# Moving the output stores of the opening and the end from SyncE's DMA queue to GpSimd's, in a fused window-attention and MLP kernel

## The chip, the cores and the metric

One core of one Trainium2 chip. The metric is device time in microseconds (us) of one execution. The trace of an execution gives the span from its first to its last instruction; the time of that same execution is about 1.7 us longer than its span.

The profile's names: PE is TensorE, DVE VectorE, ACT ScalarE, POOL GpSimd, SP SyncE. Of TensorE's work, `h_ps` is the first MLP layer, `o_ps` the second, `sc` and `pv` are the two products of attention, `tp` transposes. The granted clock is the share of TensorE's full clock that the records of a trace show. GELU is ScalarE's activation of the first layer. In these traces a DMA tells of its landing by 16 increments of a semaphore, a counter that engines wait for.

## The reference

Attention over a window of 32 positions to each side, 8 batches of 8 heads, 576 positions, head size 64, and then a two-layer MLP on the 4608 tokens that come out:

```python
def _attn_ref(q, k, v):                       # (8, 8, 576, 64) each
    scores = np.matmul(q, k.transpose(0, 1, 3, 2)) / np.sqrt(64)
    mask = np.abs(pos[:, None] - pos[None, :]) <= 32
    ...                                       # masked softmax
    return np.matmul(attn, v)

def _moe_ref(x, w_in, w_out):                 # x (4608, 512), w_in (512, 2048), w_out (2048, 512)
    h = x @ w_in
    g = h * (1.0 / (1.0 + np.exp(-1.702 * h)))
    return (g @ w_out).astype(np.float32)
```

## The kernel before

Tokens are handled in 36 units of 128. After an opening ("head") that fills the pipeline, each "window" computes attention for two units, the first layer for two units before them and the second layer for two more. An output tile `o_sb` (128 x 512, float32) is stored in two DMAs of 128 KB. Inside the kernel the rows are permuted by four (`JT = 4`), so a store's access pattern starts with a dimension of 4:

```python
    def stores(self, eng):
        while self.o_sb:
            u, o_sb = self.o_sb.pop(0)
            row = 128 * u + 32
            for blk in range(2):
                eng.dma_start(self.out[row + 64 * blk:row + 64 * blk + 64, :].rearrange("(s j) f -> j s f", j=JT),
                                  o_sb[64 * blk:64 * blk + 64])
```

The windows of the steady state store through GpSimd (52 DMAs). SyncE (SP) stores units 0 to 3 in the opening (8 DMAs) and units 30 to 34 at the end (10). SP also issues all DMA transposes, in program order; the one of key block 12 comes right behind the opening's stores:

```python
        run(1)
        self.stores(nc.sync)          # units 0 to 3, on SP
        self.load_v(8)                # loads are issued by GpSimd
        self.load_v(9)
        self.load_v(10)
        self.load_k(12)
        self.load_heads(3, "q")
        self.layer1(2, 0)
        ...
        self.load_v(11)
        self.load_v(12)
        self.load_k(13)
        self.keys_X(12)               # nc.sync.dma_start_transpose(self.kT[...], ...)
```

The last unit (`layer2_last`) stores each half as soon as it is copied, through SP and ScalarE. That is not changed.

The softmax here doesn't subtract the row's maximum and nothing guards it: scores larger than these inputs give would overflow.

Of the kernel before, what the change touches and what calls it, by code (L numbers as in the profile page):

```python
# [21 lines left out]
JT = 4  # L22
# [5 lines left out]
class _Kernel:  # L28
# [305 lines left out]
            self.cast(eng or nc.vector, o_sb, o_ps)  # L334
            self.o_sb.append((u, o_sb))

    def stores(self, eng):
        while self.o_sb:
            u, o_sb = self.o_sb.pop(0)
            row = 128 * u + 32  # L340
            for blk in range(2):
                eng.dma_start(self.out[row + 64 * blk:row + 64 * blk + 64, :].rearrange("(s j) f -> j s f", j=JT),  # L342
                                  o_sb[64 * blk:64 * blk + 64])

    def layer2_last(self):

# [26 lines left out]
    def head(self):  # L373

        nc, dve, act, pool = self.nc, self.nc.vector, self.nc.scalar, self.nc.gpsimd
# [91 lines left out]
        def run(n):  # L467
            for _ in range(n):
                l2.pop(0)()
# [23 lines left out]
        run(1)  # L493
        self.x_T(5, "a", act)
        run(1)
        self.stores(nc.sync)
        self.load_v(8)
        self.load_v(9)
        self.load_v(10)
        self.load_k(12)  # L500
        self.load_heads(3, "q")
        self.layer1(2, 0)
        self.values(6)
        self.norm(6)
# [15 lines left out]
    def window(self, w):  # L520
        nc, dve, sp = self.nc, self.nc.vector, self.nc.sync
        a, b = 2 * w, 2 * w + 1
        att = w < self.NW
        eng = {0: dve, 1: nc.scalar}
        l2 = [(lambda u=u, i=i: self.layer2(u, i, "oa"[u % 2] if w == self.NW else "oh"[u % 2], eng[u % 2]))
              for u in (2 * w - 4, 2 * w - 3) for i in range(4) if u < self.NU - 1]
        l1 = [(lambda d=d: self.layer1(w - 1, d)) for d in range(8)] if w <= self.NW else []

        def run(lst, n=1):
            for _ in range(min(n, len(lst))):  # L530
                lst.pop(0)()

        def loads():
            for m in (2 * w + 4, 2 * w + 5):
                if 12 < m < self.NU:
                    self.keys_X(m)
            for m in (2 * w + 5, 2 * w + 6):
                if m < self.NU:
                    self.load_v(m)
                if m + 1 < self.NU:  # L540
                    self.load_k(m + 1)
            if w % 2 == 0 and 512 * (w // 2 + 2) < self.N:
                self.load_heads(w // 2 + 2, "q")

        if w == 4:
            self.scores(7)
            self.scores(a)
            run(l2, 3)
            self.band(7)
            self.scores(b)  # L550
            run(l2)
            self.band(a)
            self.values(7)
            self.norm(7)
            self.gelu_table()
            self.band(b)
            run(l2, 2)
            self.values(a)
            run(l2)
            self.values(b)  # L560
            self.x_T(7, "t", nc.scalar)
            self.norm(a)
            self.x_T(a)
            self.norm(b)
            self.x_T(b)
            loads()
            self.keys_wrap()
            run(l2)
            run(l1, 2)
            for hp in range(4):  # L570
                self.pair_heads("q", 3, hp, dve)
            run(l1, 2)
            for hp in range(4):
                self.queries_T(3, hp, "t", nc.scalar)
                run(l1)
            self.feed(w)
            return
        self.stores(nc.gpsimd if att else nc.sync)
        loads()
        if att:  # L580
            self.scores(a)
            if w > 5:
                self.scores(b)
        run(l2, 2)
        if w == 5:
            self.scores(b)
        run(l2)
        if att:
            self.gelu_table()
            self.band(a)  # L590
            self.band(b)
        run(l2)
        run(l2, 2)
        if att:
            self.values(a)
            self.values(b)
            self.norm(a)
            self.x_T(a)
            self.norm(b)
            self.x_T(b)  # L600
        run(l2, 0 if w == self.NW else 2)
        if w > self.NW:
            self.stores(nc.sync)
            self.layer2_last()
        run(l1, 4)
        self.feed(w)
        run(l1, 4)
        run(l2, 2)
        if w >= self.NW - 1:
            self.stores(nc.sync)  # L610

    def feed(self, w):

# [68 lines left out]
```

## Time and profile before

| | before |
|---|---|
| time, median of 3 runs | 318.3 us (318.05 to 319.51) |
| span of the traced run, and its time | 314.7 us, 316.4 us |
| TensorE busy | 95% |
| chain that ended last | TensorE 89% |
| opening stores on SP | 8, issued from 52.0 us |
| end stores on SP | 10, the last two from 306.64 us |

TensorE is the bound: a change in DMA traffic shows in the time only where TensorE waits for it. Two lines of SP's timeline are added here, because the prediction read them wrongly (columns: start us, duration us, engine, line, operation, tiles, count):

```profile
52.00 7.46 SPq L342 DMA_DIRECT2D out_dram<-o_sb  x8
59.57 4.74 SPq L148 DMA_TRANSPOSE kT<-kn  x1
```

The second is the key transpose. Its issue starts as soon as the eight stores are issued and takes 4.74 us, where most later transposes take 1.2 to 1.6.

### The profile page before, as it was taken

How to read it: one execution, taken by the hardware profiler on the slowest of the kernel's cores; microseconds unless marked ns; L12 is line 12 of the kernel's file. 1: busy time of each engine (PE TensorE's matmuls, PEld its weight loads, DVE VectorE, ACT ScalarE, POOL GpSimd, SP SyncE). 2: the span in 40 equal slices, each digit the busy share in tenths (PEclk: the TensorE clock that was granted, in tenths of full speed). 3: DMA queues.
4: the chain of work that ended last, by engine and by line, in shares of the span. 5: the costliest groups of instructions: out<-in, count | busy, mean ns of one | idle time of the engine just before them, and what ended most of it. 6: DMA issues, size and time to landing. Idle time of an engine off the chain costs nothing.

```text
span 314.7 us, 8731 instructions
## 1 busy us (share of the span) xinstructions
PE 298.3 (95%) x3719; PEld 205.0 (65%) x3754; DVE 122.4 (39%) x373; ACT 189.0 (60%) x302; POOL 120.4 (38%) x173
## 2 busy tenths in 40 slices
PE   7999999995999999999999999999999999999993
PEld 4678655852857585858584848585858575757762
DVE  3581068454335334442435252616160707070001
ACT  3476364790785757566666667676757575765330
POOL 8993455413616361736171617161612202000000
PEclk9999999997999999999999999999999999999999
DMA  7999999999996999899989999999999222202103
GB/s 130 154 193 200 196 188 177 178 85 133 107 83 110 154 162 118 121 151 181 97 125 131 182 114 126 142 192 92 130 136 124 49 57 52 52 19 73 46 21 79
DMA packets 128238, 38.22 MB, mean 121 GB/s; under 512 B 108744, under 2 KB 125384, under 8 KB 128200
## 3 DMA queue, kind: packets, MB, share of 16 engines
q0 software_dynamic: 87424, 25.08, 89.3%
q1 hardware_dynamic: 40680, 12.53, 33.0%
q8 instruction: 29, 0.48, 0.7%
q10 hardware_dynamic: 96, 0.07, 0.1%
q14 instruction: 9, 0.07, 0.1%
HBM read 36.96 MB, written 9.44 MB: 147 GB/s over the span
## 4 chain that ended last, share of the span: by engine, by line
PE 89%; ACT 4%; issue 3%; DVE 1%; DMA 1%; ACTq 0%
PE h_ps L319 39%; PE o_ps L330 37%; PE sc L244 4%; PE pv L280 3%; PE tp L168 2%; PE junk L370 1%; PE o_ps L356 1%; DMA k_raw<-in_k_dram 1%; ACT p L252 1%; ACT qT L103 1%; ACT p L250 1%; ACT g L321 1%; PE tp L307 1%; PE tp L165 1%; DVE x L292 1%
## 5 line engine op out<-in xcount | busy, mean ns | idle before, releaser
L319 PE MATMUL h_ps<-xT,w_in_sb 128*128 128x256 bf16 x1152 | 130.9, 273 | 0.0
L330 PE MATMUL o_ps<-w_out_sb,g 128*128 128x512 bf16 x525 | 122.9, 381 | 7.9 <-issue 7.5
L319 PEld LDWEIGHTS <-w_in_sb 128*128 128x128 bf16 x1152 | 111.8, 98 | 16.7 <-DVE xT L103 0.3
L321 ACT ACTIVATE g<-h_ps 128x512 bf16<-128x512 f32 x144 | 85.9, 597 | 45.6 <-PE h_ps L319 45.5
L330 PEld LDWEIGHTS <-g 128*128 128x128 bf16 x560 | 51.6, 98 | 61.4 <-issue 4.3
L342 POOL DMA_DIRECT2D out_dram<-o_sb x52 | 33.1, 640 | 114.6 <-DVE o_sb L103 77.3
L264 DVE TENSOR_TENSOR p<-p,mask 128x512 bf16<-128x512 bf16 (+1 forms) x74 | 30.0, 413 | 101.8 <-ACT p L250 99.2
L137 POOL DMA_DIRECT2D ve<-in_v_dram x40 | 34.8, 875 | 12.4 <-DMA w_out_sb<-in_moe_w_out_dram 4.0
L250 ACT ACTIVATE p<-sc 128x512 bf16<-128x512 f32 (+1 forms) x74 | 36.7, 579 | 3.5 <-PE sc L244 3.3
L103 ACT COPY o_sb<-o_ps 128x512 f32<-128x512 f32 x15 | 8.8, 586 | 38.7 <-PE o_ps L330 38.7
L292 DVE TENSOR_TENSOR x<-pv,rec 128x256 bf16<-128x256 f32 x72 | 30.6, 425 | 2.5
L144 POOL DMA_DIRECT2D kn<-in_k_dram x27 | 23.6, 879 | 8.0 <-DMA ve<-in_v_dram 5.3
L103 DVE COPY o_sb<-o_ps 128x512 f32<-128x512 f32 x20 | 13.6, 686 | 24.4 <-PE o_ps L330 24.4
L291 DVE RECIPROCAL rec<-pv 128x4 f32<-128x4 f32 x72 | 12.6, 175 | 20.1 <-PE pv L280 20.1
L250 ACT ACT_TABLE_LOAD x15 | 19.2, 1283 | 0.3
L364 ACT ACT_TABLE_LOAD x14 | 18.0, 1283 | 0.2
L280 PEld LDWEIGHTS <-p 128*64 128x64 bf16 x576 | 11.4, 113 | 9.1 <-issue 7.1
L103 DVE COPY kT<-tp 128x512 bf16<-128x512 bf16 (+1 forms) x13 | 8.5, 659 | 21.4 <-PE tp L168 20.7
L103 ACT COPY qT<-tp 128x512 bf16<-128x512 bf16 (+1 forms) x16 | 9.1, 572 | 11.8 <-PE tp L168 10.7
L131 POOL DMA_DIRECT2D qs<-in_q_dram x17 | 12.3, 732 | 8.6 <-DMA ve<-in_v_dram 5.0
L244 PEld LDWEIGHTS <-kT 64*64 64x64 bf16 x1152 | 11.9, 108 | 5.3 <-issue 4.9
L244 PE MATMUL sc<-qT,kT 64*64 64x64 bf16 x1152 | 14.4, 196 | 0.2
(59 smaller groups left out, 142.5 us busy)
## 6 DMA issues: line engine op xcount, KB each, us to landing
out_dram<-o_sb POOLq DMA_DIRECT2D x52, 128.0 KB, 5.3
ve<-in_v_dram POOLq DMA_DIRECT2D x32, 128.0 KB, 8.8
kn<-in_k_dram POOLq DMA_DIRECT2D x21, 128.0 KB, 9.2
out_dram<-o_sb SPq DMA_DIRECT2D x18, 128.0 KB
w_in_sb<-in_moe_w_in_dram POOLq DMA_DIRECT2D x4, 512.0 KB, 7.8
w_out_sb<-in_moe_w_out_dram POOLq DMA_DIRECT2D x4, 512.0 KB, 11.5
qs<-in_q_dram POOLq DMA_DIRECT2D x2, 448.0 KB, 14.4
qs<-in_q_dram POOLq DMA_DIRECT2D x3, 256.0 KB, 6.0
```

The lines of the kernel that those rows point to most:

```text
L103: (eng.copy if eng is self.nc.scalar else eng.tensor_copy)(out, in_)
L137: self.nc.gpsimd.dma_start(self.ve[m % NV][off:off + n, :, :self.D], self.v[b, :, s:s + n, :].rearrange("h s d -> s h d"))
L144: self.nc.gpsimd.dma_start(kn[off:off + n], self.k[b, :, s:s + n, :].rearrange("h s d -> s h d"))
L244: nc.tensor.matmul(sc[eo][lo:lo + 64, n, :], self.kT[r, hp, at:at + 64], self.qT[r, JT * hp:JT * hp + JT, q0:q0 + 16], start=(hp in (0, hp ...
L250: nc.scalar.activation(p[:, eo, cols], sc[eo][:, cols], AF.Exp, scale=self.scale)
L264: self.nc.vector.tensor_mul(pv, pv, msk.to_broadcast([128, len(hps), 2, SQ]))
L280: nc.tensor.matmul(acc[half][blk * 64:blk * 64 + 64, hh, :], p[:, h % 2, h // 2 * 2 + blk, :], vt[:, h, :D + 1], start=(hh == 0), stop=(hh ...
L292: nc.vector.tensor_mul(x[:, hs, :], acc[half][:, :, :D], rec[:, hs, :].to_broadcast([128, 4, D]))
L319: nc.tensor.matmul(hps[:, i, :], self.w_in_sb[:, kr, ff * 128:(ff + 1) * 128], self.xT[t][:, kr, :], start=(i == 0 and kr == 0), stop=(i = ...
L321: nc.scalar.activation(self.g[t][:, 2 * d:2 * d + 2, :], hps, AF.Gelu_apprx_sigmoid)
L330: nc.tensor.matmul(o_ps, self.g[t][:, ff, s * 128:(s + 1) * 128], self.w_out_sb[:, ff, :], start=(ff == 0), stop=(ff == self.NFF - 1))
L342: eng.dma_start(self.out[row + 64 * blk:row + 64 * blk + 64, :].rearrange("(s j) f -> j s f", j=JT), o_sb[64 * blk:64 * blk + 64])
```

## The change

The intent: SP's queue carries only transposes and the last unit, and the stores of opening and end go the way that the steady state's stores go. In the opening the call also moves behind five loads, because GpSimd issues in order and would otherwise hold them until the first tile is ready.

```diff
-    def stores(self, eng):
+    def stores(self):
...
-                eng.dma_start(self.out[row + 64 * blk:row + 64 * blk + 64, :].rearrange("(s j) f -> j s f", j=JT),
-                                  o_sb[64 * blk:64 * blk + 64])
+                self.nc.gpsimd.dma_start(self.out[row + 64 * blk:row + 64 * blk + 64, :].rearrange("(s j) f -> j s f", j=JT),
+                                         o_sb[64 * blk:64 * blk + 64])
@@ the opening
-        self.stores(nc.sync)
         self.load_v(8)
         self.load_v(9)
         self.load_v(10)
         self.load_k(12)
         self.load_heads(3, "q")
+        self.stores()
@@ the windows
-        self.stores(nc.gpsimd if att else nc.sync)
+        self.stores()
...
         if w > self.NW:
-            self.stores(nc.sync)
+            self.stores()
...
         if w >= self.NW - 1:
-            self.stores(nc.sync)
+            self.stores()
```

## The prediction

> **What bounds the kernel now.** I read the page first (busy shares, 40 slices, chain), then the chain of waits around the one slice in which TensorE is not full, then the DMA view of the stretches before and in it, then the span's end.
>
> ```profile
> PE 298.3 (95%) x3719; PEld 205.0 (65%) x3754; DVE 122.4 (39%) x373; ACT 189.0 (60%) x302; POOL 120.4 (38%) x173
> ...
> PE   7999999995999999999999999999999999999993
> ...
> PEclk9999999997999999999999999999999999999999
> ```
>
> TensorE (PE) is busy 95% of the span and carries 89% of the chain, so most DMA work is hidden. But one slice, the tenth (70.8 to 78.7 us), has PE at 5 tenths with a granted clock of 7 tenths. The chain there, in order of time (start, us, what):
>
> ```profile
> 69.90 1.24 PE o_ps L330 x5
> 71.14 3.23 issue
> 74.38 0.71 PE o_ps L330 x2
> 75.09 0.58 PE pv L280 x16
> 75.67 1.82 PE o_ps L330 x4
> 77.49 0.58 PE pv L280 x8
> ```
>
> PE stands still for 3.23 us and waits for no semaphore ("issue"). After it the same work is slow: 16 pv matmuls take 0.58 us, before it 0.38. The table by stretch (PE busy first, clock, DMA share and GB/s last) says why:
>
> ```profile
> 66.00:71.00 5.00, 4.84 (x67) 2.19 (x66) 2.47 (x8) 4.96 (x9) 0.85 (x1) 1.00 1.59 71
> 71.00:74.40 3.40, 0.17 (x2) 0.02 (x2) 1.50 (x5) 0.17 (x1) 1.83 (x3) 1.00 2.10 85
> 74.40:77.00 2.60, 2.60 (x22) 1.04 (x22) 1.12 (x4) 0.00 (x0) 0.84 (x2) 0.57 1.32 147
> 77.00:79.30 2.30, 2.25 (x27) 1.33 (x27) 1.33 (x6) 0.59 (x1) 0.00 (x0) 0.75 1.48 202
> ```
>
> So the standstill also costs clock. What is an "issue" wait in mid-stream? In the DMA view, the instruction queue q8 moves nothing from 59.6 to 71.0 us, and its next packet lies in 71 to 73. First 59.6 to 71, then 71 to 73:
>
> ```profile
> DMA packets 3266, 1.22 MB, mean 107 GB/s; under 512 B 2875, under 2 KB 2875, under 8 KB 3266
> ## 3 DMA queue, kind: packets, MB, share of 16 engines
> q0 software_dynamic: 2377, 0.30, 96.1%
> q1 hardware_dynamic: 889, 0.92, 75.6%
> ```
>
> ```profile
> q8 instruction: 1, 0.02, 5.7%
> ```
>
> In the raw packets that fetch of 16 KB runs from 71.08 to 72.90 us (1.82 us; the 11 others between 12 and 122 us take 0.89 to 1.17). PE had started about 450 instructions since the last fetch, against 235 and 262 before the two earlier fetches: it had run dry. The instruction some 256 past the last fetch started at 64.9 us, so I take the fetch as about 6 us late.
>
> What held it? In 64 to 71 us q0 moves only 0.05 MB and q1 0.48 MB, while the DMA engines count as busy. q1 holds the eight opening stores that SP issued from 52.0 to 57.2 us, and behind them SP's first key transpose, issued at about 63.8 us, once its wait for TensorE's key transposes had ended. In the trace's semaphore events the eight stores land at 59.4, 61.0, 62.7, 64.4, 66.1, 67.8, 69.5 and 71.4 us, one each 1.7 us, and only 4 of each semaphore's 16 increments come late; the transpose lands at 72.6 to 74.0. Transpose packets of up to 7.8 us start between 63 and 66 us: I read them as engines held until the store-laden four reach their part. POOL's loads issued from 52 on take twice their usual 9 us to land:
>
> ```profile
> ve<-in_v_dram POOLq DMA_DIRECT2D x1, 128.0 KB, 18.5
> kn<-in_k_dram POOLq DMA_DIRECT2D x2, 64.0 KB, 19.0
> ```
>
> **What the Trainium skill says.** "DMA: Bandwidth & Descriptors", section "Why a DMA increments its semaphore by 16 and not by 1": a DMA is spread over the largest number of engines up to 16 that divides the slowest dimension of its access pattern; from a hardware queue they are always the lowest-numbered ones, from GpSimd a cursor moves on from transfer to transfer. The store's slowest dimension is j = 4. The trace agrees for SP: 4 late increments, and 128 KB in 1.7 us is 77 KB/us. For POOL it fits, no more: there 128 KB land 5.3 us (median) after issue, with two pairs in flight, without such a queue. The same page, "SWDGE vs HWDGE vs iDMA": the two kinds feed different queues inside each DMA engine, which takes turns between them; so stores on POOL do not stand ahead of the SP transpose. "TensorE: Matmul & The Clock Gate", Part 1: after an idle window of about 3.4 us the clock halves, and comes back after a busy one. The trace agrees: a record of clock 0.5 from 74.8 for 3.4 us, after 3.23 us of standstill.
>
> **The change part by part.** Order of instructions: PE, DVE and ACT unchanged; POOL gets 8 stores behind the loads of queries 3 and 10 stores at the end; SP loses 18.
>
> (1) Opening, SP. The eight stores leave q1. The transpose still issues at about 63.8 (its wait is for PE and DVE) but finds its queue empty; later transposes take 4 to 8 us to land, so it lands at about 69. The fetch comes in time. Removed: 3.23 us of standstill. Clock: the work from 74.38 to 79.32 is 10 o_ps (10 x 0.243, from 0.97 for 4 = 2.43), 2 x 16 pv (0.76) and 4 transposes (0.22): 3.4 us at full clock against 4.94, so 1.5; by the clock column 2.6 x 0.43 + 2.3 x 0.25 = 1.7. I take 1.6. Nothing in that stretch waits for other data: the probabilities (DVE until 72.5) are the latest input, needed at about 73. Sum: 4.8 us, all on the path, because PE's work afterwards is back to back.
>
> (2) Opening, POOL. Eight issues of 0.64 us = 5.1 us. The first waits for its tile until 52.0, as on SP. POOL has eight completion semaphores in turn, so each DMA waits for the one eight before; with the landings seen, the stores issue at about 52.0, 52.7, 53.8, 54.4, 55.2, 56.4, 57.1 and 59. The next load (values 11), issued at 49.85 before, then waits for the first store to land: about 60, some 10 us later. But the queue ahead of it holds only 1 MB, at the 160 to 190 KB/us of this stretch about 6 us: values 11 and 12 land at about 66 and 67 (before: 65.7 and 71.5), keys 13 at about 68 (before 73). First users: DVE's odd-value copies at 80.06, about 75 afterwards. Slack 8 us; cost 0.
>
> (3) End. Units 30 to 33 store long before the end: 0. Unit 34's two stores go by SP at 306.64 and 307.22, land at 310.7 and 312.6, and sit on the same four engines as parts of the last stores (issued at 309.87). Of those, the increments come by 312.7 but for the last two or three, at 313.2 to 313.5; the closing waits follow. POOL starts a store about 0.29 us after its tile's copy ends (247.01 to 247.30; SP 0.03), so 306.9 and 307.5, and its pairs land 3.5 to 4.5 us after issue: 310.4 to 312.0. The four engines are free, and the last increment comes at about 312.7 to 312.9. Gain 0.6 (0 to 0.8).
>
> Sum: 4.8 + 0.6 = 5.4. From 318.3 that is 312.9; I add 0.3 for small waits elsewhere: **313.2 us**.
>
> **The rivals.** (a) The standstill belongs to the transpose, not to the stores ahead of it: any first transpose under full load queues blocks the fetch. For it: q0 is full then. Against: the other transposes under load (80 to 92 us) leave PE running. Then only the end gains: 317.6. (b) The 10 us later loads become the wait: DVE's copies at 75 or the key transpose 13 stop. For: the three loads before these took 10 to 11 us to land. Against: 8 us of slack. It would give back 1 to 4 us: 314 to 317. (c) POOL's slower path sets the end: its stores land after the last unit's, up to +0.5 us. Against: they are issued 2.4 us sooner. (d) More than I count: fetches elsewhere also speed up. The other "issue" waits of PE at this line are 4.3 us in 27 pieces, 0.16 us each on average, pipeline rather than fetch; at most 1 us, so 312.
>
> **Range and chances.** The main term is two-sided: it is there (4 to 5.5 us) or, by (a), not at all; I give (a) and (b) together about 1 in 6, mostly in part. Before's three runs spread 1.5 us. Range 311.9 to 316.0. Faster by over 2% needs under 311.9, a gain of 6.4 us, more than I can find: 0.11. Slower by over 2% needs a new stall of over 6 us: 0.02. Within 2%: 0.87.
>
> **What would show it.** Right: no "issue" piece over 1 us in the chain at 60 to 80 us, the tenth slice back at 9 in PE and its clock, an instruction fetch between 63 and 68 us, loads issued after the opening stores landing in about 8 us and not 18, the span shorter by about 5 us with nearly all of it gained before 80 us. Wrong: the standstill still there at another place (a), DVE or SP waiting for ve or kn loads near 75 us (b), or the final waits ending on a POOL store (c).

## The result, and the profile after

| | before | changed |
|---|---|---|
| time, median of 4 runs each | 318.56 us (318.05 to 319.51) | 311.37 us (310.64 to 311.81) |
| span of the traced run | 314.7 us | 308.9 us |
| mean granted clock of the traced run | 0.993 | 0.997 |

The ratio is 0.9768, with a 95% interval of 0.9738 to 0.9799: faster by 2.3%. Ratios here are the mean time of one kernel's fast runs over that of the other's in the same rounds, so not quite the ratio of the medians quoted. A second comparison (below) gave 0.9796 (0.976 to 0.983): that the changed kernel is faster is clear in both, that it is so by over 2% only in the first. The predicted 313.2 us was too high, and 311.37 lies just under the range.

The page of the changed kernel, the lines for TensorE and its clock:

```profile
PE   7999999999999999999999999999999999999994
...
PEclk9999999999999999999999999999999999999998
```

The hole in the tenth slice is gone, in TensorE and in its clock. The chain of the changed kernel at the same place (start, us, what):

```profile
70.13 1.67 PE o_ps L330 x7
71.80 0.38 PE pv L280 x16
72.18 0.97 PE o_ps L330 x4
73.15 0.38 PE pv L280 x16
73.52 0.33 PE tp L307 x4
```

There is no "issue" piece, and both groups of 16 pv matmuls take 0.38 us. The table by stretch (stretch, TensorE's busy time second, then clock, DMA share and GB/s last):

```profile
71.00:74.40 3.40, 3.35 (x47) 1.76 (x47) 3.23 (x13) 0.89 (x3) 0.92 (x2) 1.00 1.04 168
74.40:77.00 2.60, 2.60 (x24) 2.24 (x24) 2.48 (x12) 1.76 (x4) 1.37 (x3) 1.00 0.55 126
```

Where TensorE had 0.17 us of work in 3.4 us it now has 3.35, at full clock in both stretches. The DMA view of 59.6 to 71 us of the changed kernel:

```profile
q0 software_dynamic: 8033, 1.47, 156.5%
q1 hardware_dynamic: 202, 0.04, 4.9%
q8 instruction: 1, 0.02, 0.5%
...
ve<-in_v_dram POOLq DMA_DIRECT2D x3, 128.0 KB, 5.8
kn<-in_k_dram POOLq DMA_DIRECT2D x2, 128.0 KB, 4.9
```

GpSimd's queue q0 moves 1.47 MB where it moved 0.30, the loads land in 5 to 6 us where those of the same blocks took 16 to 19, and the instruction fetch (q8) lies inside the stretch: in the raw packets from 66.45 to 67.44 us. SP's timeline from 50 to 66 us has one line (columns: start us, duration us, engine, line, operation, tiles, count):

```profile
56.30 2.18 SPq L148 DMA_TRANSPOSE kT<-kn  x1
```

The transpose issues 3.3 us sooner, and its longest packet there takes 1.5 us, not 7.8.

Comparing the two traces, the end of VectorE's last copy moved from 309.84 to 305.21 us, 4.63 us sooner, nearly all of it gained before 80 us; from there to the end of the span it takes 3.71 us instead of 4.86. Together that is the 5.8 us between the spans. But the timed runs differ by 7.2 us. Why they differ by more than the traces is the question that the experiments had to settle, beside that of the cause.

### The profile page after: what moved, and what is told of

Its sections match the earlier page's. It is cut to its first block, busy times and chain, and to the rows that moved or that the text cites. A ratio compares the mean times of both kernels' runs of the same rounds, so it can differ in the third digit from the quotient of the medians.

```text
span 308.9 us, 8727 instructions
## 1 busy us (share of the span) xinstructions
PE 296.8 (96%) x3719; PEld 204.5 (66%) x3754; DVE 122.9 (40%) x373; ACT 188.9 (61%) x302; POOL 131.9 (43%) x191
## 4 chain that ended last, share of the span: by engine, by line
PE 90%; ACT 3%; issue 2%; DMA 2%; DVE 1%; POOL 0%; POOLq 0%; ACTq 0%
PE h_ps L319 40%; PE o_ps L330 37%; PE sc L244 4%; PE pv L280 3%; PE tp L168 2%; DMA ks<-in_k_dram 2%; PE junk L370 1%; PE o_ps L356 1%; ACT qT L103 1%; ACT p L250 1%; ACT g L321 1%; DVE p L269 1%; PE tp L307 1%; DVE x L292 1%; ACT L250 0%
## 5 line engine op out<-in xcount | busy, mean ns | idle before, releaser
L342 POOL DMA_DIRECT2D out_dram<-o_sb x70 | 44.2, 636 | 150.3 <-DVE o_sb L103 83.7
L280 PE MATMUL pv<-vo,p 128*64 128x65 bf16 x288 | 13.5, 196 | 0.2 <-DVE p L269 0.2
```

Of the source, the lines that this page charges most:

```text
L280: nc.tensor.matmul(acc[half][blk * 64:blk * 64 + 64, hh, :], p[:, h % 2, h // 2 * 2 + blk, :], vt[:, h, :D + 1], start=(hh == 0), stop=(hh ...
L342: self.nc.gpsimd.dma_start(self.out[row + 64 * blk:row + 64 * blk + 64, :].rearrange("(s j) f -> j s f", j=JT), o_sb[64 * blk:64 * blk + 64])
```

## The experiments

Theory A: the opening's stores run on four DMA engines, the key transpose queued behind them holds the others, the instruction fetch comes late, TensorE runs dry and loses clock; the loss differs from run to run. Its rivals are named in the expectations. Beside the comparison above there were 12 runs, seven of them of new kernels. All results were correct. They fall into three groups, on three different chips; each group shares its own runs of before. No ratio of theirs is clear of the 2% mark: they are read for whether there is a gain, and the traces for its cause. The cuts of code compare with the kernel before, those of stores_ahead and after_dve with the changed kernel.

One stretch measures the standstill and its aftermath cleanly: from the start of the opening's last GELU (the 24th) to the start of the next (the 25th), read from the timeline of each trace. The table has it for all traces; "standstill" is the time for which TensorE does nothing near 71 us, "half clock" is the time at half clock in mid-kernel.

| trace | span | 24th to 25th GELU | standstill | half clock | last copy to end |
|---|---|---|---|---|---|
| before (of the prediction) | 314.7 | 15.53 | 3.23 | 3.4 | 4.86 |
| before_again | 315.0 | 15.06 | 2.69 | 3.4 | 4.64 |
| before_look | 313.3 | 14.56 | 2.14 | 3.4 | 4.98 |
| before_look2 | 316.1 | 17.37 | 4.06 | 6.8 | 4.89 |
| before_look3 | 318.4 | 16.76 | 4.33 | 3.4, and 3.4 at 20 us | 4.58 |
| end_only | 313.1 | 15.02 | 2.67 | 3.4 | 3.88 |
| changed | 308.9 | 10.70 | none | none | 3.71 |
| after_again | 309.0 | 10.71 | none | none | 3.93 |
| opening_only | 311.2 | 10.71 | none | 3.4 at 20 us | 4.66 |
| transpose_first | 310.2 | 10.70 | none | none | 4.89 |
| sp_spread | 310.1 | 10.71 | none | none | 4.90 |
| stores_ahead | 310.7 | 10.70 | none | none | 4.05 |
| after_dve | 310.0 | 10.71 | none | none | 3.87 |
| transpose_later | 324.4 | 10.71 | 10.25 later | 13.7 | 4.84 |

### before_again: no edit, a null comparison and a new trace

> The kernel before, unchanged, with a new trace. Theory A (the standstill of TensorE near 71 us and the halved clock after it vary from run to run, and the trace that the prediction used was a lucky one: 316.4 us, where the timed runs took 318.1 to 319.5): spans of about 316 to 318 us, mean granted clock at or below 0.993, and a new trace with a standstill of 3.2 to 5 us or a second stretch at half clock. Rival B (the timed runs are longer by something outside the opening): the same 3.2 us of standstill and 3.4 us at half clock, and the missing 1.5 to 2 us elsewhere.

Measured: 317.26 us (316.7 to 319.8, 4 runs) beside 318.49 (314.74 to 320.51, 7 runs) of the same kernel: ratio 1.0068, interval 0.997 to 1.016. Two samples of one kernel differ by 0.7% here, and single runs by up to 1.8%. The granted clock goes with it: the runs of before in this group had 0.981 to 0.997, the fastest of them the highest. Three of the seven were marked slow, because they lie over 1.5% above the fastest, and left out of the ratio. On one core that mark cannot tell a disturbed run from a long standstill, so the ratios of this group are biased against the kernels compared. By the means of all seven runs of before (318.15 us) the ratios would be 0.999 here, 0.987 for opening_only and 0.992 for end_only. The trace itself was again a short one (315.0 us), and its standstill of 2.69 us lies under the 3.2 to 5 that theory A gave: neither answer yet.

### opening_only

```diff
-    def stores(self, eng):
+    def stores(self, eng=None):
+        eng = eng or self.nc.gpsimd
...
-        self.stores(nc.sync)
         self.load_v(8)
...
         self.load_heads(3, "q")
+        self.stores()
```

> Only the opening's eight stores move to GpSimd (behind the loads, as in the change); the ten at the end stay on SyncE. Theory A: the larger part, 4.6 us by the two traces and 6 us against the timed runs of before, so about 312.5 us (ratio 0.981); no standstill. Rival B (the end is worth more than the traces show): a gain of 4.5 us or less, about 314 us.

Measured: 313.82 us beside 318.49, ratio 0.9937 (0.987 to 1.000) with the three slow runs of before left out; the medians differ by 4.7 us. The number is nearer to rival B's 314 us than to the 312.5 of theory A. But the trace has no standstill, and the stretch takes 10.71 us, as in the changed kernel. It also has a stretch at half clock at 20 us, after waits for the first weights, which is not of this change, and from the last copy to the end it takes 4.66 us, so that no more than about 1 us is left for the end. The opening is the larger part; the sum cannot be told closer from this group.

### end_only

```diff
-        self.stores(nc.gpsimd if att else nc.sync)
+        self.stores(nc.gpsimd)
...
-            self.stores(nc.sync)       # two calls at the end
+            self.stores(nc.gpsimd)
```

> Only the ten stores at the end move to GpSimd. By the two traces the stretch after VectorE's last copy shrinks from 5.28 to 4.1 us: theory A expects a gain of 1.2 us, 317.3 us (ratio 0.996), with the standstill near 71 us still there. Rival B: 2.5 us or more, 316 us or less.

Measured: 314.81 us (314.27 to 318.79), ratio 0.9991 (0.988 to 1.010). The median lies 3.7 us under that of before, as rival B has it, while the ratio without the three slow runs shows nothing: the time alone decides nothing here. The trace does: the stretch still takes 15.02 us with a standstill of 2.67 us, and from the last copy to the end it takes 3.88 us, as in the changed kernel (3.71, 3.93), not 4.58 to 4.98 as in the five traces of before (the expectation counts from that copy's start). So the end is worth about 1 us, and has nothing to do with the standstill. This trace also shows a fetch being held: in the raw packets it starts at 63.93 us and ends at 72.10, 8.2 us, where fetches elsewhere take about 1; the transpose's packets there end at 72.12.

### transpose_later

```diff
         self.load_k(13)
-        self.keys_X(12)
...
                 if 12 < m < self.NU:
+                    if m == 13:
+                        self.keys_X(12)
                     self.keys_X(m)
```

> All stores stay on SyncE where they are in the kernel before; only the key transpose of block 12 is issued later, beside that of block 13, so that no transpose stands in SyncE's queue behind the eight opening stores. Theory A (the stores fill four DMA engines' rings, and the transpose behind them holds the other twelve, with the loads and the instruction fetch, until the four are done): the other engines keep moving loads in 60 to 71 us (well over the 0.05 MB of before in 64 to 71), the fetch comes by 68 us, no standstill, a gain of 4 to 6 us (313 us). Rival C (the stores alone hold up the fetch, by sitting on the engine that carries it): the fetch still comes at about 71 us, the standstill of 3 us stays, 318 us.

Measured: 323.27 us, ratio 1.0242 (1.014 to 1.034), slower: a miss in the time, for a reason that I had overlooked. The chain of this kernel:

```profile
75.15 1.72 DMA out_dram<-o_sb
76.87 10.60 DMA kT<-kn
```

VectorE's copy of the wrapped keys needs the transpose that I had put off, and the transpose, now issued from 76.9 us among others, is done only after 87; TensorE stands still for 10.25 us behind the copy, and the clock is halved for 13.7 us. On the question asked it still answers: the stores stayed on SP, no transpose stood behind them, the fetches started at 63.9 and 70.0 us, and there was no standstill at 71 us. The loads moved 0.18 MB in 64 to 71 us, more than the 0.05 of before but not much. That speaks against rival C. As the time is spoilt by a wait of my own making, a cleaner test followed.

### after_again: the changed kernel, with runs of before from the same chip

> The changed kernel again, beside the kernel before on the same chip, with the granted clock of every run. Theory A (the gain is the standstill, 3 us, plus a halved clock after it that differs from run to run, plus 1.2 us at the end): changed runs at a mean clock of 0.993 to 0.998 and 310.5 to 312.5 us, runs of before spread over 314.5 to 320.5 us and lower clocks (0.981 to 0.997), longer the lower; ratio about 0.979. Rival B (the first comparison was a matter of the chip or of chance): the changed kernel's runs spread as widely as those of before and as low in clock, ratio 0.985 or above.

Measured: 311.38 us (310.72 to 311.91, 6 runs) beside 317.97 (315.42 to 319.33, 11 runs), ratio 0.9796 (0.976 to 0.983). The changed kernel's clock was 0.997 to 1.000, that of before 0.985 to 0.998. So the gain holds in a second comparison, the changed kernel varies much less than the kernel before, and rival B falls.

### transpose_first: the stores stay on SP, the transpose goes ahead of them

```diff
         run(1)
-        self.stores(nc.sync)
         self.load_v(8)
...
         self.keys_X(12)
+        self.stores(nc.sync)
```

> All stores stay on SyncE, but the first key transpose is issued ahead of the eight opening stores instead of behind them, so that it meets an empty queue. Theory A (transpose behind the stores holds the engines that have no stores): the transpose lands near 62 us, the fetch comes by 68 us, no standstill near 71 us, and about 4 to 5 us less than before, 313 us; the stores still land one each 1.7 us until about 72. Rival C (the stores alone hold up the fetch): the fetch still at about 71 us, standstill of about 3 us, 317 to 318 us.

Measured: 312.43 us (311.48 to 313.48), ratio 0.9827 (0.979 to 0.986): as theory A has it, against 317 to 318 by rival C. SP's timeline of this kernel:

```profile
56.75 1.30 SPq L148 DMA_TRANSPOSE kT<-kn  x1
58.11 6.80 SPq L342 DMA_DIRECT2D out_dram<-o_sb  x8
```

The same nine DMAs from the same queue, in the other order. The stores still land one each 1.7 us, from 64.5 to 77.7 us, on four engines. They also go out 6 us later than before; that this is not the reason, transpose_later shows, where they went out from 51.7 us and the fetches came in time. The DMA view of 64 to 71 us, first of the kernel before, then of this one:

```profile
q0 software_dynamic: 361, 0.05, 98.9%
q1 hardware_dynamic: 329, 0.48, 61.3%
```

```profile
q0 software_dynamic: 1830, 0.52, 72.1%
q1 hardware_dynamic: 266, 0.51, 21.2%
q8 instruction: 1, 0.02, 0.8%
```

The kernel before moved 0.05 MB of loads and no instruction. Here ten times as much goes through, and a fetch. Some loads are still as late as before (queries 4 land 17 us after issue), and TensorE does not mind: the stretch takes 10.70 us. So neither the slow stores nor the late loads cost anything; what cost was the transpose behind the stores.

### sp_spread: stores on SP over all 16 DMA engines

The version cuts each of the eight opening stores into four:

```diff
+                if eng is self.nc.sync and u < 4:
+                    for j in range(JT):
+                        eng.dma_start(dst[j], src[16 * j:16 * j + 16])
+                else:
+                    eng.dma_start(dst, src)
```

> The eight opening stores stay on SyncE, ahead of the transpose, but each is cut into four, one for each j, so that its slowest dimension is 16 and all 16 DMA engines carry it. Theory A (four engines of sixteen are the cause): the stores drain as they are issued, 32 issues of about 0.5 us, done by about 68 us and not held up; the loads keep moving in 60 to 68 us, no standstill, 312.5 to 314 us although the transpose is then issued some 10 us later than in the changed kernel. Rival D (it is the hardware queue of SyncE, not the number of engines): standstill as before, 317 to 318 us.

Measured: 312.39 us (311.8 to 314.62), ratio 0.9837 (0.980 to 0.988), stretch 10.71 us, no standstill. All 16 increments of these stores' semaphores now come late, where before only 4 did. The key transpose went out at 72.4 us, 16 us later than in the changed kernel, and it cost nothing. (The last store landed at 72.7 us, not by 68 as expected.) So SP's hardware queue as such is not the trouble (rival D falls); that four engines loaded and twelve held are is the reading that fits. The edit also moves the transpose to a time when little else runs, so of the two it is the weaker proof; transpose_first is the clean one.

### before_look, before_look2, before_look3: more traces of the kernel before

> One more trace of the kernel before. Theory A: a standstill of TensorE of 2.5 to 5 us near 71 us with a late fetch in this trace too, and any mean clock below 0.993 comes with a second stretch at half clock, which the trace shows.

> A further trace of the kernel before, to see where the slower of its runs spend their time: traced so far are spans of 313.3 to 315.0 us, while timed runs go to 318. Theory A: again a standstill of 2 to 5 us near 71 us; if the span is over 316 us, more time at half clock than the one stretch of 3.4 us in mid-kernel. Rival: the same standstill and clock, and waits for loads in the first 25 us instead.

> The same as the look before it: one more draw of where the slower runs spend their time.

Measured: times of 315.02, 317.86 and 320.09 us, spans 313.3, 316.1 and 318.4. The two long ones are what was missing. Their chains at the standstill, first of before_look2, then of before_look3:

```profile
70.52 4.06 issue
74.58 1.03 PE o_ps L330 x2
```

```profile
72.64 4.33 issue
76.97 0.61 PE o_ps L330 x2
```

The standstills are 4.06 and 4.33 us, and in before_look2 the clock is halved for 6.8 us instead of 3.4, starting at 73.2 us, inside the standstill. In the raw packets the late fetch runs from 71.5 to 73.2 and from 74.0 to 75.5 us; in the short trace, before_look, from 69.7 to 71.5 with a standstill of 2.14, which is under the 2.5 to 5 expected. before_look3 is long for other reasons too, which are not of this change: a wait of 1.7 us for weights near 18 us, with 3.4 us at half clock after it, and a short wait at 220 us (1.07 us).

### stores_ahead: the new place in the program undone

```diff
         run(1)
+        self.stores()
         self.load_v(8)
...
         self.load_heads(3, "q")
-        self.stores()
```

> As the changed kernel, but the opening's eight stores keep their old place in the program, ahead of the loads of values 8 to 10, keys 12 and queries 3, instead of behind them. If the new place matters (GpSimd stands still until the first tile is ready near 52 us, and the loads behind it come 10 us later, past their first use near 64 us): a wait of VectorE or TensorE for these loads near 64 us and 313 us or more. Rival (the loads are far enough ahead anyway): within 1 us of the changed kernel, 311 to 312 us.

Measured: 311.02 us (310.23 to 312.44), ratio 0.9782 (0.973 to 0.983) beside 318.32 (one of those 11 runs was marked slow): the same as the changed kernel. The loads of values 8 to 10 do come later (they land at 63.9 to 65.6 us, where the kernel before has them at 53 to 55), but the stretch takes 10.70 us all the same. The move behind the loads is a precaution that costs nothing and, here, gains nothing.

### after_dve: an attempt at a faster kernel

```diff
-                self.queries_T(3, hp, "t", nc.scalar)
+                self.queries_T(3, hp, "t", dve)
```

> The changed kernel, with the four PSUM copies of query block 3 on VectorE instead of ScalarE. In the changed kernel's chain the stretch 78 to 82 us waits twice for a GELU and then the copy on ScalarE (0.60 + 0.49 us, twice), while VectorE is idle there. Expected: these four pieces leave the chain, 1 to 2 us less, 309.5 to 310.5 us. If the copies are hidden some other way: 311.4 us, the same.

Measured: 312.0 us (310.51 to 314.5), ratio 0.9817 (0.976 to 0.987): not told apart from the changed kernel. In the trace the eight GELUs from the 25th to the 32nd take 7.00 us instead of 7.46, so 0.5 us is saved where I expected 1 to 2. The pieces left ScalarE, and TensorE's own work took most of their place in the chain. No version tried is faster than the changed kernel beyond the spread of the runs.

## Why the prediction was wrong in size and right in mechanism

**What bounds, and what holds the fetch.** Right: TensorE ran dry because a fetch came late, and the stores on SP's queue with the transpose behind them were the cause. transpose_first shows it by changing nothing but their order. In all six traces with a standstill, TensorE starts again 1.3 to 1.6 us after the late fetch has ended. That the transpose's packets occupy the twelve engines without stores is argued from packet times (the longest takes 6.9 to 8.7 us in the five traces of before and in end_only, and 0.4 to 2.0 us in seven traces without a standstill); no run measured one engine by itself.

**Part 1, SP.** The step "The transpose still issues at about 63.8" was wrong. I had taken an inferred wait for TensorE at its word. The duration of the instruction itself, 4.74 us, says that it was being issued from 59.57 us, slowly, I read, because the stores had filled the queue; in the changed kernel, where nothing stands ahead of it, it issued at 56.30 and landed by 63.51, not at about 69. (The last store's issue, too, ended at 59.46 and not at 57.2.) The conclusion did not depend on it. The fetch came at 66.45 us, within the stated 63 to 68.

**Part 1, the 4.8 us.** Right for the trace it was read from: between the two traces the stretch of the table shrinks by 4.83 us (15.53 to 10.70). Wrong as the mean of the kernel before: over its five traces the stretch takes 14.56 to 17.37 us, mean 15.86, against 10.70. That is 5.15 us on average, between 3.9 and 6.7 from run to run.

**Part 2, GpSimd.** Right, nearly to the number: the stores issued between 52.5 and 58.8 us (foreseen 52.0 to 59), values 11 and 12 landed at 65.7 and 66.6 (foreseen 66 and 67), keys 13 at 67.0 (foreseen 68), and nothing waited for them. stores_ahead shows that even more delay is free.

**Part 3, the end.** Right in kind, mis-sized: foreseen 0.6 us, measured about 1 us (4.79 us on average over the five traces of before, 3.82 over the two of the changed kernel). In the first pair of traces the last increment came 3.66 us after the last copy's end before and 2.72 after, 0.94 us. SP's closing waits gave the rest: they check one semaphore after another, and before, the late ones came early in that list, with seven still to be checked.

**The sum, where it failed.** The step that failed is "From 318.3 that is 312.9; I add 0.3", with the two sizes above that went into it. It took a gain read from one trace off the median of other runs. The traced run had taken 316.4 us, under every timed run beside it (318.05 to 319.51), and that should have told me that the timed runs lose more in the opening than the traced one. With the means of the table, 5.15 + 0.97 = 6.1 us; 318.3 less that is 312.2, inside the range. The first comparison gave 7.2 us and the second 6.6. The clock speaks the same way: over 22 runs of before in two of the groups it averages 0.990, over 10 runs of the changed kernel 0.9975; a straight line through the 22 gives 3.1 us for each 0.01, so some 2.2 us of lost clock (an estimate, the tail included) where I had counted 1.6. The allowance of 0.3 us for "small waits elsewhere" had no line behind it and went the wrong way. Of the 0.5 to 1.1 us that remain, the traces hold 0.4: the mean spans, 315.5 and 308.95, differ by 6.5, of which 0.1 lies before the 24th GELU and 0.3 after the 25th, most of it the waits of before_look3 at 220 us. The rest, 0.1 to 0.7 us, stays open: the kernel before also varies in its first 64 us (the 24th GELU starts between 64.0 and 66.2 us), and five traces are too few to share that out.

**The rivals.** (a) fell: a transpose under load with no four-engine stores ahead of it (changed kernel, transpose_first) leaves TensorE running. (b) fell: no wait for loads. (c) fell: the last GpSimd store landed at 307.53 us, before the last unit's at 307.93. (d) was nearest: there was more to gain than I counted, though not from fetches elsewhere: from the 25th GELU to the last copy the first pair of traces takes 229.6 us each. The chance of 0.11 for faster by over 2% was too low for the same reason as the sum.

## What to carry to other kernels

A transfer that runs on few DMA engines is not only slow itself: a transpose that stood behind it in the same queue held up the loads and the instruction fetch here, so look for an "issue" wait without a releaser and a missing packet on the instruction queue. Put the transpose first, or give the few-engine stores another queue; here either one took the standstill away. And when the traced run is faster than every timed run beside it, trace more runs before subtracting what the one trace shows.

## What the Trainium skill lacked or had wrong

- "Runtime: NRT & Kernel Launch", section "Instruction fetch mechanics", has the fetch in blocks of 16 KiB (256 instructions) by a DMA queue of the sequencer, and calls the cost of a block boundary mostly hidden. The traces agree on the block (29 packets of 16,384 bytes on q8) but show a price when the DMA engines are held: fetches late by several us, TensorE still for 2.1 to 4.3 us in five traces, and 3.4 to 6.8 us at half clock after or in them.
- "DMA: Bandwidth & Descriptors", sections "Queues, rings and completion order" and "Why a DMA increments its semaphore by 16 and not by 1", explain rings and the number of engines, and the trace agrees: 4 late increments for the stores on SP, 16 when they are cut by four. Neither says what a transpose behind a four-engine DMA on the same queue does to the other twelve: 0.05 MB of loads moved in 64 to 71 us, against 0.52 MB with the transpose ahead of the same stores, and 4.74 us to issue it, against 1.30.
- "TensorE: Matmul & The Clock Gate", Part 1, halves the clock after an idle window of about 3.4 us. The stretches measured in mid-kernel are multiples of 3.4 us, as it says, but four of the six standstills are shorter (2.14 to 3.23 us) and brought one all the same: a window need not be wholly idle, and how much idle time in one is enough the page does not say.
